# Regrouping the small-tile bursts of a fused attention and gated MLP kernel on one NeuronCore

## The chip, the cores and the metric

The kernel runs on one core of a Trainium2 chip. Five engines work beside each other, each through its own list of instructions in order: TensorE (PE, matmuls; its weight loads are listed as PEld), VectorE (DVE), ScalarE (ACT), GpSimd (POOL) and SyncE (SP, which issues DMAs; here POOL issues DMAs too). They wait for each other by semaphores. The metric is the device time of one execution in microseconds (us), lower is better. All times below are us unless they say otherwise.

## The reference

Two attentions one after the other, and then a gated layer. There are 8 batches, 8 heads, 576 rows of 64 numbers, and 32 "packed" queries p for each head.

```
packed = softmax(p k^T / 8) v           # 32 x 64 for each head
attn   = softmax(q packed^T / 8) packed # 576 x 64 for each head
x      = attn with the heads side by side      # 4608 x 512
h      = x w_in                                # 4608 x 2048
out    = (h * cos(h)) w_out                    # 4608 x 512
```

## The kernel before

All matmuls are in bf16. x is never formed. For one batch, the packed result of each head is multiplied with that head's 64 rows of w_in. That gives PPW, 256 rows (8 heads x 32 packed rows, in two halves y of 128) by 2048 columns. With a2n, the normalised second attention, h is then a2n^T PPW: a contraction over 256.

The work of one batch b has these parts, each a function:

- `s1` (L142): first scores, 16 matmuls of 64x32 tiles (L137, in `scores`), and two exponentials on ACT (L146), which write a1.
- `a1_xbar` (L158) or `a1_pe` (L163): a1 is transposed to a1T, by a DMA or by PE.
- `pp` (L173): the packed product, 48 matmuls of 96x32 tiles with 64 columns (L180); two copies take it to pp_sb. `pp_T` (L188): two transposes (L192) and a copy to ppT.
- `ppw(b, n)` (L195): 512 columns of PPW, eight matmuls of 64x32 tiles with 512 columns (L207). The result lies in a two-bank PSUM tile and is copied to PPW by the engine that is named ("evacuated"), or by two engines, one half each.
- `s2` (L221): second scores, 16 matmuls of 64x32 tiles (L137), two exponentials to a2u (L225).
- `sums2` (L228): the sums over the packed rows, two matmuls (L233), and a logarithm on ACT (L235). `normalise` (L238): exp(-log sum) on ACT (L241) and a2n on DVE (L243).
- `h_mm(b, fc)` (L248), for each of 16 groups fc of 128 columns: four matmuls of 288 columns (L254) into a two-bank tile, the cosine on ACT (L258), the product h cos h into gT on DVE (L261). I call it a step, and its fc its column.
- `out_gen` (L331): the output of a batch in chunks of 128 rows, 16 accumulating matmuls of 512 columns each (L339), a copy to osb (L343) by `osb_eng`, and DMAs on SP's queue (L345). Four chunks, or five for odd batches, whose fifth chunk holds the last 64 rows of two batches (`joint`).

The tiles of 64x32 and 96x32 use a part of the array each, so that 8 or 4 of these matmuls run side by side. All others use the whole array.

The order on each engine is the order in which the code is written (`manual_schedule`). The output matmuls of the batch before are the filler: `fill(n)` (L355) writes the next n of them wherever it is called. A slot (`slot`, L471) is the 16 steps of one batch; after each step it fills a share of the output matmuls that are left, and hooks put other work behind given columns. The argument `keep` leaves some output matmuls over, and `heavy` gives a column a larger share. `set_filler(b)` (L350) first writes out everything that is left of the batch before.

Around the slots, for batch s from 3 on (L545 to L576): what is left of the filler, `s2(s)`, ppw n=2, 8 output matmuls, `s1(s+1)`, ppw n=3, transposes by DMA, the two `sums2` with output matmuls between, `normalise`, 13 output matmuls, then the slot. In it `pp(s+1)` stands behind column 5, `pp_T(s+1)` behind column 6, and `pw2(s+1)`, which is ppw n=0 and n=1 of the next batch, behind column 10. The slots of batches 1 and 2 are laid out by hand (L496, L542), and batch 0 is a special case: its steps are `h_one` (L274), with one bank each and 512 rows; its last 64 rows are done in `h_rest` (L286), a hook in slot 1 that uses one two-bank tile for 32 matmuls, one cosine and one product over 1024 columns.

PSUM: the pool psA has three two-bank tiles, which all of s1, s2, sums2, pp, pp_T, ppw and h_mm share; the pool psO has two banks for the output chunks. Which of the three places a new tile gets is settled when the program is built, and its first matmul waits until the engines that read the old content are done. In the part of batch 0 with `h_one` psA is replaced by six single banks (psH).

ACT has two function sets, one with the exponential and logarithm, one with the cosine; `preload_act_table_set` loads one (ACT_TABLE_LOAD). Before slot 1 ACT's order is: the cosines of batch 0, the copy of ppT, the load of the set for the exponential (L449), its copy of the transposed q of batch 1 (qT, one of three groups; DVE copies the other two), then s2(1).

Of the kernel before, what the change touches and what calls it, by code (L numbers as in the profile page):

```python
# [15 lines left out]
def kernel(  # L16
# [72 lines left out]
    def psa(dt=FP32):  # L89
        return psum["A"].tile([128, 2, 512 if dt == FP32 else 1024], dt, name="psA", tag="A")  # L90
# [9 lines left out]
    def one(dt=FP32):  # L100
        return psum["H"].tile([128, 512 if dt == FP32 else 1024], dt, name="psH", tag="H")
# [56 lines left out]
    def a1_xbar(b):  # L158
        t = a1T[b] = att_pool.tile([128, 2, C, 128], BF16, name="a1T", tag="a1T")
        nc.sync.dma_start_transpose(out=t.rearrange("p a c x -> p (a c) x"),  # L160
                                    in_=a1[b % 2].rearrange("p a c x -> p (a c x)"))
# [11 lines left out]
    def pp(b, eng=V, own=None):  # L173

        ps = own() if own else psa()[:, 0, :]
        for y in range(2):
            for j in range(C):
                c = 2 * (j % 3) + j // 3
                for x in range(4):
                    nc.tensor.matmul(ps[32 * x:32 * x + 32, y * D:(y + 1) * D],  # L180
                                     a1T[b][0:TP, y, j, 32 * x:32 * x + 32],
                                     bf["v", b][:, 2 * x + y, c * D:(c + 1) * D],
                                     start=(j == 0), stop=(j == C - 1))
        t = pp_sb[b % 2].rearrange("p a d -> p (a d)")
        copy(eng, t[:, 0:2 * D], ps[:, 0:2 * D])
        copy(eng, t[:, 2 * D:3 * D], ps[:, 0:D])
# [58 lines left out]

    gT, joint = {}, {}

    def h_mm(b, fc):  # L248
        if fc == 0:
            g_tile(b)  # L250
        ps = psa()
        for y in range(2):
            for e in range(2):
                nc.tensor.matmul(ps[:, e, 0:HS], PPW[b][:, y, fc * 128:(fc + 1) * 128],  # L254
                                 a2n[b][:, y, e * HS:(e + 1) * HS], start=(y == 0), stop=(y == 1))
        cs = cos_pool.tile([128, S], BF16, name="cosT")
        csv = cs.rearrange("p (e x) -> p e x", e=2)
        ACT.activation(out=csv, in_=ps[:, :, 0:HS], func=AF.Sin, bias=PI_HALF)  # L258

        def rest():  # L260
            V.tensor_tensor(out=gT[b][:, fc, :].rearrange("p (e x) -> p e x", e=2),  # L261
                            in0=ps[:, :, 0:HS], in1=csv, op=ALU.mult)
            if fc % 8 == 7:
                j0 = (b % 2) * 64
                G.tensor_copy(out=joint[b // 2][:, fc - 7:fc + 1, j0:j0 + 64],  # L265
                              in_=gT[b][:, fc - 7:fc + 1, 512:576])
        return rest
# [3 lines left out]
        if b % 2 == 0:  # L271
            joint[b // 2] = j_pool.tile([128, NFC, 128], BF16, name="joint", tag="joint")

    def h_one(b, fc):  # L274

        if fc == 0:
            g_tile(b)
        ps = one()
        for y in range(2):
            nc.tensor.matmul(ps, PPW[b][:, y, fc * 128:(fc + 1) * 128], a2n[b][:, y, 0:512],  # L280
                             start=(y == 0), stop=(y == 1))
        cs = cos_pool.tile([128, 512], BF16, name="cosT")
        ACT.activation(out=cs, in_=ps, func=AF.Sin, bias=PI_HALF)  # L283
        V.tensor_tensor(out=gT[b][:, fc, 0:512], in0=ps, in1=cs, op=ALU.mult)  # L284

    def h_rest(b):  # L286

# [28 lines left out]
    def n_chunks(b):  # L316
        return 5 if b % 2 and b < B - 1 else 4
# [13 lines left out]
    def out_gen(b):  # L331
        groups = [(0, 1), (2,), (3,)] if b == 0 else [(c,) for c in range(n_chunks(b))]
        for grp in groups:
            pss = {c: O.tile([128, DM], FP32, name="ot", tag="ot") for c in grp}
            for f0 in range(0, NFC, 4):
                for c in grp:
                    for fc in range(f0, f0 + 4):
                        w = joint[b // 2][:, fc, :] if c == 4 else gT[b][:, fc, c * 128:(c + 1) * 128]
                        nc.tensor.matmul(pss[c], w, w_out_bf[:, fc, :],  # L339
                                         start=(fc == 0), stop=(fc == NFC - 1))  # L340
                        if fc == NFC - 1:
                            osb = o_pool.tile([128, DM], FP32, name="osb")
                            copy(osb_eng[0], osb, pss[c])  # L343
                            for a, z, rows in pieces_of(b, c):
                                nc.sync.dma_start(out=rows, in_=osb[a:z, :])  # L345
                        yield

    filler = [None, 0]

    def set_filler(b):  # L350
        fill(1000)
        filler[0] = out_gen(b)
        filler[1] = 16 * n_chunks(b)

    def fill(n):  # L355
        while n > 0 and filler[1] > 0:
            next(filler[0])
            filler[1] -= 1
            n -= 1

    def load_w_in(n):
# [11 lines left out]
    def warm(n, wps=None, w=None):  # L373
        wps, w = bank() if wps is None else wps, wz if w is None else w
        for _ in range(n):
            nc.tensor.matmul(wps, w[:, 0:128], w, start=True, stop=True)  # L376
# [60 lines left out]
    banks(0)  # L437
    a1_pe(1, own=one)
    recips(1)
    for fc in range(NFC):  # L440
        h_one(0, fc)
        if fc in (0, 4, 8):
            ppw(0, 1 + fc // 4, (ACT, ACT if fc == 8 else V), own=True)
        if fc == 13:
            pp(1, ACT, own=bank)
    warm(2)
    pp_T(1, ACT, own=bank)
    warm(2)
    ACT.preload_act_table_set(EXP_SET)  # L449
    pe_T("q", 1, (ACT, V, V), own=one)  # L450
    warm(4)
    load("v", 2)
    load("q", 2)
    load("k", 3)
# [2 lines left out]
    set_filler(0)  # L457
    s2(1)
    ppw(1, 0, V)
    fill(1)  # L460
    sums2(1, 0)
    fill(1)
    sums2(1, 1)
# [5 lines left out]
    fill(7)  # L469

    def slot(s, hooks, keep=0, heavy={}):  # L471
        left = filler[1] - keep
        weight = [1 + heavy.get(fc, 0) for fc in range(NFC)]
        for fc in range(NFC):
            h_mm(s, fc)()
            quota = (left * sum(weight[:fc + 1])) // sum(weight) - (left + keep - filler[1])
            first = quota
            while hooks and hooks[0][0] == fc:
                if first == quota and fc in heavy:
                    first = quota // 2  # L480
                    fill(first)
                hooks.pop(0)[1]()
            fill(quota - first if first != quota else quota)

    def pw2(b, n=0, eng=None):
        ppw(b, n, eng)
        ppw(b, n + 1, eng)

    def tk(n, b, i):
        return lambda: pe_T(n, b, (ACT, V, ACT), (i,))  # L490

    def cross(n, b):
        return lambda: xbar(n, b)

    osb_eng[0] = ACT
    slot(1, [(2, lambda: ppw(1, 2, (ACT, V))), (4, lambda: h_rest(0)),  # L496
             (5, lambda: ppw(1, 3, (ACT, V))), (6, lambda: pack_p(2, 4)), (8, tk("k", 2, 0)), (9, tk("k", 2, 1)),
             (9, cross("q", 2)), (10, tk("k", 2, 2)), (12, cross("k", 3))], 4, {4: 2})
    ACT.preload_act_table_set(EXP_SET)
    osb_eng[0] = V  # L500
    G.tensor_copy(out=gate, in_=xT["k", 3][0:1, 0, 0:1])
# [1 line left out]
    load("q", 3)  # L503
    load("k", 4)

    fill(1000)
    set_filler(1)
    s1(2)
    fill(7)
    a1_pe(2, (0,))  # L510
# [2 lines left out]
    recips(2)  # L513
    fill(5)
    pp(2)
    fill(2)
    pp_T(2)
    s1(3)
    a1_xbar(3)
    recips(3)  # L520
    fill(6)
    s2(2)
    ppw(2, 0, V)
    xbar("q", 3)
    xbar("k", 4)
    fill(1)
    sums2(2, 0)
    fill(3)
    sums2(2, 1)
# [7 lines left out]
    G.tensor_copy(out=gate, in_=xT["k", 4][0:1, 0, 0:1])  # L537
    for n, b in (("v", 4), ("q", 4), ("k", 5)):
        load(n, b)
    fill(9)  # L540
    osb_eng[0] = ACT
    slot(2, [(3, lambda: ppw(2, 2, (ACT, V))), (6, lambda: ppw(2, 3, (ACT, V))),  # L542
             (7, lambda: pp(3, ACT)), (8, lambda: pp_T(3, ACT)), (11, lambda: pw2(3))], 5, {11: 3})

    for s in range(3, B):  # L545
        nxt = s + 1 < B
        ACT.preload_act_table_set(EXP_SET)
        osb_eng[0] = V
        fill(1000)
        set_filler(s - 1)  # L550
        s2(s)
        ppw(s, 2, V)
        fill(8)
        if nxt:
            s1(s + 1)
            ppw(s, 3, V)
            a1_xbar(s + 1)
            xbar("q", s + 1)
            recips(s + 1)
            if s + 2 < B:  # L560
                xbar("k", s + 2)
                G.tensor_copy(out=gate, in_=xT["k", s + 2][0:1, 0, 0:1])
        else:
            ppw(s, 3, V)
        fill(4)
        sums2(s, 0)
        fill(5)
        sums2(s, 1)
        normalise(s)
        ACT.preload_act_table_set(SIN_SET)  # L570
        fill(13)
        osb_eng[0] = ACT
        for n, b in (("v", s + 2), ("q", s + 2), ("k", s + 3)):
            if b < B:
                load(n, b)
        slot(s, [(5, lambda: pp(s + 1, ACT)), (6, lambda: pp_T(s + 1, ACT)), (10, lambda: pw2(s + 1))] if nxt else [], 5, {10: 3})  # L576
    set_filler(B - 1)
    fill(1000)
    tail_chunk(B - 1, 4)
# [30 lines left out]
```

## Time and profile before

| | us |
|---|---|
| median of three runs | 249.68 (249.47 to 250.37) |
| the profiled execution | 249.53 |
| its span in the profile | 247.6 |
| PE busy, of the span | 234.0 |
| ACT busy | 170.3 |
| DVE busy | 158.5 |

The span is the time from the first to the last instruction of the program that the profile holds; some 1.9 us of the execution lie around it. The granted clock of TensorE was full throughout. In a line of a timeline stand the start, the time from the start of the first to the end of the last of its instructions, the engine, the source line, the operation, out<-in, the shape, the number of instructions, and in brackets the engine's idle time ahead of it with what ended it. Matmuls overlap: the next starts while the last drains, so the distance between starts is the cost of one, not its length. The records of some matmuls are missing in the trace, mostly the first output matmul after a burst of small tiles.

### The profile page before, as it was taken

What the parts mean: (1) busy time and instruction counts of PE and PEld (TensorE: products, weight loads), DVE (VectorE), ACT (ScalarE), POOL (GpSimd) and SP (SyncE); (2) the same over time, 40 slices, a digit from 0 to 9 for tenths busy, and PEclk for the clock granted to TensorE, in tenths of its full rate; (3) what the DMA queues carried; (4) which work ended last, traced back from release to release, by engine and by line L of the source; (5) the groups of instructions that cost most, each with busy time, mean ns of one, the idle gap of its engine ahead of it and who ended that gap; (6) DMA issues with size and microseconds to landing.
All of it is one profiled execution on the core that took longest, in us unless ns stands there. A gap on an engine that the chain in (4) does not pass through costs nothing.

```text
span 247.6 us, 5423 instructions
## 1 busy us (share of the span) xinstructions
PE 234.0 (95%) x2204; PEld 128.3 (52%) x2240; DVE 158.5 (64%) x244; ACT 170.3 (69%) x284; POOL 38.2 (15%) x61
## 2 busy tenths in 40 slices
PE   7988889999989999999999999999999999999993
PEld 3453344566445554565446554565456554665452
DVE  3369977676549777578757666578756685774000
ACT  2369998677568777888787677978886685874110
POOL 8532330200400041005000500030000000000000
PEclk9999999999999999999999999999999999999999
DMA  6999999999899999996999894989292113111123
GB/s 88 204 209 209 202 208 228 202 235 176 135 186 173 218 146 201 189 221 122 215 214 197 148 222 109 184 172 203 63 187 59 42 45 84 43 34 53 52 75 85
DMA packets 63992, 37.37 MB, mean 151 GB/s; under 512 B 36592, under 2 KB 59376, under 8 KB 63968
## 3 DMA queue, kind: packets, MB, share of 16 engines
q0 software_dynamic: 23184, 18.81, 50.0%
q1 hardware_dynamic: 40624, 18.09, 35.6%
q8 instruction: 17, 0.28, 0.5%
q10 hardware_dynamic: 160, 0.13, 0.2%
q14 instruction: 7, 0.06, 0.1%
HBM read 37.22 MB, written 9.44 MB: 188 GB/s over the span
## 4 chain that ended last, share of the span: by engine, by line
PE 82%; DMA 6%; DVE 4%; ACT 3%; issue 2%; POOL 2%; DVEq 0%; ACTq 0%; POOLq 0%
PE ot L339 48%; PE psA L254 22%; DMA w_in_bf<-in_moe_w_in_dram 6%; PE psA L207 3%; PE psA L137 2%; PE ot L325 1%; PE psA L233 1%; PE psA L180 1%; DVE gT L284 1%; PE psH L280 1%; DVE PPW L87 1%; ACT a2u L225 1%; DVE gT L261 1%; POOL kbf L94 1%; ACT L449 1%
## 5 line engine op out<-in xcount | busy, mean ns | idle before, releaser
L339 PE MATMUL ot<-w_out_bf,gT 128*128 128x512 bf16 x482 | 128.2, 379 | 2.8 <-issue 1.9
L261 DVE TENSOR_TENSOR gT<-psA,cosT 128x576 bf16<-128x576 f32 x112 | 83.5, 757 | 32.4 <-ACT cosT L258 31.5
L258 ACT ACTIVATE cosT<-psA 128x576 bf16<-128x576 f32 x112 | 73.0, 653 | 26.4 <-PE psA L254 24.8
L254 PE MATMUL psA<-a2n,PPW 128*128 128x288 bf16 x448 | 73.2, 286 | 0.0
L339 PEld LDWEIGHTS <-gT 128*128 128x128 bf16 x512 | 47.3, 98 | 43.5 <-issue 7.8
L254 PEld LDWEIGHTS <-PPW 128*128 128x128 bf16 x448 | 43.8, 98 | 30.5 <-issue 1.0
L87 DVE CAST PPW<-psA 128x1024 bf16<-128x1024 f32 (+1 forms) x25 | 26.1, 1050 | 7.7 <-PE psA L207 6.0
L87 DVE COPY osb<-ot 128x512 f32<-128x512 f32 (+1 forms) x14 | 9.4, 671 | 21.3 <-PE ot L325 17.4
L85 ACT COPY osb<-ot 128x512 f32<-128x512 f32 (+1 forms) x23 | 13.2, 575 | 13.5 <-PE ot L339 12.4
L265 POOL COPY joint<-gT 128x512 bf16<-128x512 bf16 x14 | 8.6, 617 | 88.4 <-DVE gT L261 88.4
L243 DVE SCALAR_TENSOR_TENSOR a2n<-a2u,r,lns 128x576 bf16<-128x576 bf16 x16 | 12.4, 814 | 8.1 <-ACT lns L241 8.1
L146 ACT ACTIVATE a<-psA 128x576 bf16<-128x576 f32 x16 | 10.3, 646 | 8.3 <-PE psA L137 8.3
L235 ACT ACTIVATE lns<-psA 128x576 f32<-128x576 f32 x16 | 10.3, 651 | 6.5 <-PE psA L233 5.9
L339 PE MATMUL ot<-w_out_bf,joint 128*128 128x512 bf16 x47 | 12.6, 379 | 0.1
L376 PE MATMUL ot<-wz 128*128 128x512 bf16 (+1 forms) x23 | 10.2, 548 | 2.0 <-DVE wz L390 1.7
L225 ACT ACTIVATE a2u<-psA,rs 128x576 bf16<-128x576 f32 x16 | 11.0, 738 | 1.5 <-PE psA L137 1.4
L207 PE MATMUL psA<-w_in_bf,ppT 64*32 64x512 bf16 x224 | 10.4, 380 | 0.2
L284 DVE TENSOR_TENSOR gT<-psH,cosT 128x512 bf16<-128x512 f32 x16 | 9.9, 682 | 0.4 <-ACT cosT L283 0.4
L241 ACT ACTIVATE lns<-lns 128x576 f32<-128x576 f32 x16 | 10.0, 674 | 0.0
L85 ACT CAST PPW<-psA 128x1024 bf16<-128x1024 f32 (+1 forms) x9 | 7.4, 825 | 2.8 <-PE psA L207 2.8
L283 ACT ACTIVATE cosT<-psH 128x512 bf16<-128x512 f32 x16 | 8.7, 619 | 0.9 <-issue 0.4
L280 PE MATMUL psH<-a2n,PPW 128*128 128x512 bf16 x30 | 7.9, 381 | 0.9 <-DVE PPW L87 0.6
(90 smaller groups left out, 163.8 us busy)
## 6 DMA issues: line engine op xcount, KB each, us to landing
kbf<-in_k_dram POOLq DMA_DIRECT2D x8, 576.0 KB, 13.5
vbf<-in_v_dram POOLq DMA_DIRECT2D x8, 576.0 KB, 7.4
qbf<-in_q_dram POOLq DMA_DIRECT2D x8, 576.0 KB, 10.6
out_dram<-osb SPq DMA_DIRECT2D x24, 192.0 KB, 2.8
out_dram<-osb SPq DMA_DIRECT2D x22, 128.0 KB, 2.9
w_in_bf<-in_moe_w_in_dram POOLq DMA_DIRECT2D x4, 512.0 KB, 16.6
w_out_bf<-in_moe_w_out_dram POOLq DMA_DIRECT2D x4, 512.0 KB, 21.2
out_dram<-osb SPq DMA_DIRECT2D x26, 64.0 KB, 2.1
```

The costliest lines, as they stand in the source:

```text
L85: ACT.copy(out=out, in_=in_)
L87: eng.tensor_copy(out=out, in_=in_)
L146: ACT.activation(out=a1[b % 2][:, y, :, 0:TP].rearrange("p (e m) x -> p e m x", e=2), in_=ps[y][:, :, 0:HS].rearrange("p e (m x) -> p e m ...
L207: nc.tensor.matmul(ps[y][32 * x:32 * x + 32, :], ppT[b % 2][r, 0, x, :], w_in_bf[r, x, n * 512:(n + 1) * 512], start=True, stop=True)
L225: ACT.activation(out=a2u[b][:, y].rearrange("p (e x) -> p e x", e=2), in_=ps[y][:, :, 0:HS], func=AF.Exp, scale=rs1[b][:, y:y + 1])
L243: V.scalar_tensor_tensor(out=a2n[b][:, y], in0=a2u[b][:, y], scalar=r1[b][:, y:y + 1], in1=lns[b][:, y], op0=ALU.mult, op1=ALU.mult)
L254: nc.tensor.matmul(ps[:, e, 0:HS], PPW[b][:, y, fc * 128:(fc + 1) * 128], a2n[b][:, y, e * HS:(e + 1) * HS], start=(y == 0), stop=(y == 1))
L258: ACT.activation(out=csv, in_=ps[:, :, 0:HS], func=AF.Sin, bias=PI_HALF)
L261: V.tensor_tensor(out=gT[b][:, fc, :].rearrange("p (e x) -> p e x", e=2), in0=ps[:, :, 0:HS], in1=csv, op=ALU.mult)
L280: nc.tensor.matmul(ps, PPW[b][:, y, fc * 128:(fc + 1) * 128], a2n[b][:, y, 0:512], start=(y == 0), stop=(y == 1))
L284: V.tensor_tensor(out=gT[b][:, fc, 0:512], in0=ps, in1=cs, op=ALU.mult)
L339: nc.tensor.matmul(pss[c], w, w_out_bf[:, fc, :], start=(fc == 0), stop=(fc == NFC - 1))
```

## The change

- The slots of batches 2 to 6 have one burst of small tiles: `tiled(b)` writes ppw n=2 and n=3 of the slot's own batch and then the packed product of the next batch. The packed product has no tile of its own; it is written into unused columns (288 to 512 of the second bank) of the tile of the step just done (`spare`). ACT evacuates ppw n=2; DVE takes pp_sb's two copies and then ppw n=3. Eight output matmuls (seven in slot 2) stand ahead of this burst and three behind it. `pp_T` moves to column 11, its copy on ACT as before.
- ppw n=0 and n=1 of a batch now stand with `s2` and `s1` ahead of its own slot, evacuated by DVE, where n=2 and n=3 stood; ahead of slot 7 there are n=1, 2 and 3 in a row.
- In slot 1 ppw n=2 and n=3 stand together behind column 2; `h_rest` moves from column 4 to column 5.
- Before slot 2, `s1(3)` directly follows `pp(2)`, with `pp_T(2)` three output matmuls later; the counts of output matmuls around are shifted.
- The filler is a list: `set_filler` no longer writes out what is left, and `fill` goes on into the next batch. Slots keep 5 or 13 output matmuls over, so that slots 3 to 7 have 37 each (before: 29 in slots 3, 5 and 7, 45 in slots 4 and 6); slot 2 has 29 (before 37), slot 1 has 47 (before 48). Ahead of slot 1 there are 13 (before 12).
- In batch 0's part, ACT's copies of pp_sb now follow the cosine of column 12, column 15 uses a bank of psO, ppT is copied behind cosine 13, and ACT's group of q1's transposes is copied ahead of the load of the set for the exponential. DVE copies its two groups ahead of its last product. Eight warming matmuls become seven.

The diff, cut to its core:

```
-    def h_one(b, fc):
+    def h_one(b, fc, own=None):
...
-        ps = one()
+        ps = (own or one)()
...
-    filler = [None, 0]
+    filler = []
     def set_filler(b):
-        fill(1000)
-        filler[0] = out_gen(b)
-        filler[1] = 16 * n_chunks(b)
+        filler.append([out_gen(b), 16 * n_chunks(b)])
...
-    for fc in range(NFC):
-        h_one(0, fc)
+    for fc in range(13):
+        h_one(0, fc)()()
         if fc in (0, 4, 8):
             ppw(0, 1 + fc // 4, (ACT, ACT if fc == 8 else V), own=True)
-        if fc == 13:
-            pp(1, ACT, own=bank)
-    warm(2)
+    c13 = h_one(0, 13)
+    pp(1, ACT, own=bank)
+    c13()()
+    c14 = h_one(0, 14)
+    c15 = h_one(0, 15, own=bank)
     pp_T(1, ACT, own=bank)
-    warm(2)
+    c14()()
+    rest15 = c15()
+    warm(4, one())
+    pe_T("q", 1, (ACT, V, V), (0,), own=one)
     ACT.preload_act_table_set(EXP_SET)
-    pe_T("q", 1, (ACT, V, V), own=one)
-    warm(4)
+    pe_T("q", 1, (ACT, V, V), (1, 2), own=one)
+    rest15()
+    warm(3, one())
...
     ppw(1, 0, V)
-    fill(1)
+    fill(2)
     sums2(1, 0)
...
+    def tiled(b):
+        own, later = spare[0], []
+        for n in (2, 3):
+            later += ppw(b, n, (ACT, V)[n - 2], later=True)
+        later[0]()
+        pp(b + 1, V, own=lambda: own)
+        later[1]()
...
-    slot(1, [(2, lambda: ppw(1, 2, (ACT, V))), (4, lambda: h_rest(0)),
-             (5, lambda: ppw(1, 3, (ACT, V))), (6, lambda: pack_p(2, 4)), (8, tk("k", 2, 0)), (9, tk("k", 2, 1)),
-             (9, cross("q", 2)), (10, tk("k", 2, 2)), (12, cross("k", 3))], 4, {4: 2})
+    slot(1, [(2, lambda: pw2(1, 2, (ACT, V))), (5, lambda: h_rest(0)), (6, lambda: pack_p(2, 4)), (8, tk("k", 2, 0)), (9, tk("k", 2, 1)),
+             (9, cross("q", 2)), (10, tk("k", 2, 2)), (12, cross("k", 3))], 4, {5: (3, 3)})
...
     pp(2)
-    fill(2)
-    pp_T(2)
     s1(3)
     a1_xbar(3)
+    fill(3)
+    pp_T(2)
     recips(3)
-    fill(6)
+    fill(5)
     s2(2)
     ppw(2, 0, V)
...
-    fill(1)
+    fill(3)
     sums2(2, 0)
...
-    fill(9)
+    fill(7)
     osb_eng[0] = ACT
-    slot(2, [(3, lambda: ppw(2, 2, (ACT, V))), (6, lambda: ppw(2, 3, (ACT, V))),
-             (7, lambda: pp(3, ACT)), (8, lambda: pp_T(3, ACT)), (11, lambda: pw2(3))], 5, {11: 3})
+    slot(2, [(6, lambda: tiled(2)), (11, lambda: pp_T(3, ACT))], 13, {6: (7, 3)})
...
-        fill(1000)
         set_filler(s - 1)
+        fill(5)
         s2(s)
-        ppw(s, 2, V)
+        ppw(s, 0, V)
         fill(8)
         if nxt:
             s1(s + 1)
-            ppw(s, 3, V)
+            ppw(s, 1, V)
...
         else:
-            ppw(s, 3, V)
+            for n in range(1, 4):
+                ppw(s, n, V)
...
-        slot(s, [(5, lambda: pp(s + 1, ACT)), (6, lambda: pp_T(s + 1, ACT)), (10, lambda: pw2(s + 1))] if nxt else [], 5, {10: 3})
+        slot(s, [(5, lambda: tiled(s)), (11, lambda: pp_T(s + 1, ACT))] if nxt else [],
+             5 if s % 2 else 13, {5: (5, 3)} if nxt else {})
```

More of the change, by code (lines that the diff above doesn't have):

```diff
@@ L246 @@
     gT, joint = {}, {}
+    spare = [None]
     def h_mm(b, fc):
@@ L251, in h_mm @@
         ps = psa()
+        spare[0] = ps[:, 1, HS:512]
         for y in range(2):
@@ L281, in h_one, with cos @@
                              start=(y == 0), stop=(y == 1))
-        cs = cos_pool.tile([128, 512], BF16, name="cosT")
-        ACT.activation(out=cs, in_=ps, func=AF.Sin, bias=PI_HALF)
-        V.tensor_tensor(out=gT[b][:, fc, 0:512], in0=ps, in1=cs, op=ALU.mult)
+        def cos():
+            cs = cos_pool.tile([128, 512], BF16, name="cosT")
+            ACT.activation(out=cs, in_=ps, func=AF.Sin, bias=PI_HALF)
+            return lambda: V.tensor_tensor(out=gT[b][:, fc, 0:512], in0=ps, in1=cs, op=ALU.mult)
+        return cos
     def h_rest(b):
@@ L346, in out_gen, with to_do @@
                         yield
-    filler = [None, 0]
+    filler = []
     def set_filler(b):
-        fill(1000)
-        filler[0] = out_gen(b)
-        filler[1] = 16 * n_chunks(b)
+        filler.append([out_gen(b), 16 * n_chunks(b)])
+    def to_do():
+        return sum(n for _, n in filler)
     def fill(n):
-        while n > 0 and filler[1] > 0:
-            next(filler[0])
-            filler[1] -= 1
+        while n > 0 and filler:
+            next(filler[0][0])
+            filler[0][1] -= 1
+            if filler[0][1] == 0:
+                filler.pop(0)
             n -= 1
@@ L471, in slot, with pw2 @@
     def slot(s, hooks, keep=0, heavy={}):
-        left = filler[1] - keep
-        weight = [1 + heavy.get(fc, 0) for fc in range(NFC)]
+        left = to_do() - keep
+        weight = [1 + heavy.get(fc, (0, 0))[0] for fc in range(NFC)]
         for fc in range(NFC):
             h_mm(s, fc)()
-            quota = (left * sum(weight[:fc + 1])) // sum(weight) - (left + keep - filler[1])
-            first = quota
+            quota = (left * sum(weight[:fc + 1])) // sum(weight) - (left + keep - to_do())
+            behind = min(quota, heavy[fc][1]) if fc in heavy else quota
+            fill(quota - behind)
             while hooks and hooks[0][0] == fc:
-                if first == quota and fc in heavy:
-                    first = quota // 2
-                    fill(first)
                 hooks.pop(0)[1]()
-            fill(quota - first if first != quota else quota)
-    def pw2(b, n=0, eng=None):
+            fill(behind)
+    def pw2(b, n, eng=None):
         ppw(b, n, eng)
         ppw(b, n + 1, eng)
+    def tiled(b):
[5 more added lines that the diff above has]
+        later[1]()
     def tk(n, b, i):
@@ L504 @@
     load("k", 4)
-    fill(1000)
     set_filler(1)
+    fill(4)
     s1(2)
@@ L548 @@
         osb_eng[0] = V
-        fill(1000)
         set_filler(s - 1)
+        fill(5)
         s2(s)
-        ppw(s, 2, V)
+        ppw(s, 0, V)
         fill(8)
```

## The prediction

> **What bounds the kernel now.** I read the page's parts 1 and 4 first, the busy shares and the chain that ended last. TensorE (PE) is busy for nearly all of the span and owns 82% of the chain. So time is won only where PE's stream gets shorter or where PE waits.
>
> ```profile
> PE 234.0 (95%) x2204; PEld 128.3 (52%) x2240; DVE 158.5 (64%) x244; ACT 170.3 (69%) x284; POOL 38.2 (15%) x61
> ...
> PE 82%; DMA 6%; DVE 4%; ACT 3%; issue 2%; POOL 2%; DVEq 0%; ACTq 0%; POOLq 0%
> ```
>
> Next comes PE's timeline (columns: start us, us, what), for the price of a burst of small tiles.
>
> ```profile
> 147.56 1.89 PE L339 MATMUL ot<-w_out_bf,joint 128*128 128x512 bf16 x8
> 149.38 0.44 PE L137 MATMUL psA<-qT,ppT 64*32 64x288 bf16 x16
> 149.63 0.40 PE L207 MATMUL psA<-w_in_bf,ppT 64*32 64x512 bf16 x8
> 149.96 1.90 PE L339 MATMUL ot<-w_out_bf,gT 128*128 128x512 bf16 x7
> ```
>
> Eight output matmuls last 1.89 and one lasts 0.379 (part 5), so one starts every (1.89 - 0.379)/7 = 0.216 us. An h step, four matmuls of 288 columns, starts every 0.49 (21.8% of the chain in pieces of 0.49). The first row's stream should end at 147.56 + 8 x 0.216 = 149.29; the burst starts at 149.38, an **edge** of 0.09. Eight small matmuls run side by side in 0.216, so the third row's end at 149.85; the next row starts at 149.96, an edge of 0.11. Elsewhere the leaving edge is up to 0.13. A burst thus costs some 0.22 beyond its stream. (The gap of 0.16 "<-issue" after some bursts, followed by one output matmul too few, is a missing record, not a wait.)
>
> What else can stop PE is its three two-bank tiles (psA). How long does an h step hold one?
>
> ```profile
> 41.63 0.65 PE L254 MATMUL psA<-a2n,PPW 128*128 128x288 bf16 x4
> ...
> 42.33 0.65 ACT L258 ACTIVATE cosT<-psA 128x576 bf16<-128x576 f32 x1 [0.27 <-PE psA L254]
> ...
> 43.01 0.76 DVE L261 TENSOR_TENSOR gT<-psA,cosT 128x576 bf16<-128x576 f32 x1 [0.16 <-ACT cosT L258]
> ...
> 43.35 0.41 PE L207 MATMUL psA<-w_in_bf,ppT 64*32 64x512 bf16 x8
> ```
>
> The product ends at 43.77, 2.14 after the step's start. The next view shows a step whose tile is taken over by the transposes of the packed product (L192), 2.18 later:
>
> ```profile
> 108.02 0.65 PE L254 MATMUL psA<-a2n,PPW 128*128 128x288 bf16 x4
> ...
> 110.20 0.27 PE L192 MATMUL psA<-ident,pp_sb 128*128 128x128 bf16 x2
> ```
>
> So a tile is free again **2.18 us** after its step's start, if ACT and DVE are not behind. PE was there at 110.06 and lost 0.14. What takes a tile out of turn brings the next steps closer to that limit.
>
> **The change, part by part** (plus is later; sums against the profiled execution, whose time is 249.53: 247.6 of span and 1.9 around it, 0.15 under the median of 249.68).
>
> *Bursts.* From 41 us on I count 29 bursts in the timeline and 20 in the changed order: one fewer in slot 1, one in the stretch before slot 2, three in slot 2, one in each of slots 3 to 6. That is -9 x 0.22 = -1.98. Six of the joined bursts change shape inside (64x32 to 96x32 or back). No row shows this switch. Its bounds are 0, as between L137 and L207, two lines of one shape (149.38 to 149.63 is their stream), and 0.22, a leaving and an entering edge. The nearest row is one edge, so I take 0.10: +0.6, with 0 and 1.3 as ends. The sums below have both terms in them.
>
> The Trainium skill, "TensorEngine Tiling (Array Packing)", Key Properties, says that a change of tiling mode drains TensorE. Each edge of 0.09 to 0.13 agrees, and by that rule the inner switch is an edge of its own, which leaves the sum as it is; if a switch of row size alone were none, the sum would be 0.6 lower.
>
> *q1 sooner.* Before slot 1 the chain runs over ACT:
>
> ```profile
> 33.23 0.42 ACT L85 COPY ppT<-ot 128x256 bf16<-128x256 bf16 x1
> 33.66 1.28 ACT L449 ACT_TABLE_LOAD   x1
> 34.95 0.80 ACT L85 COPY qT<-psH 128x768 bf16<-128x768 bf16 x1
> 36.24 1.37 ACT L225 ACTIVATE a2u<-psA,rs 128x576 bf16<-128x576 f32 x2 [0.48 <-PE psA L137]
> ```
>
> In the new order pp_sb's copies follow the cosine of column 12 (31.5 to 31.8), then come ACT's cosine 13, ppT's copy, cosines 14 and 15 (to 33.7). The transposes of q1 wait for its load, which lands at 33.12 as now (0.51 of PE's weight loads waits for it), so the copy by ACT is 33.7 to 34.5, the table load 34.5 to 35.8. DVE copies its two groups before the last product, at 34.0 to 35.05; the scores start at 35.1 and are read at 35.5. The table load is last: the first exponential starts at 35.81 instead of 36.24, -0.43. One more output matmul fits into PE's wait of 0.25 before L233 (37.03): -0.22. Together **-0.65**; bounds 0, if the load lands later, and -0.9, if the load of the table hid too.
>
> The Trainium skill, "ScalarE: Activation LUTs", What ACT_TABLE_LOAD costs, speaks against this: 1.28 and a drain of 1.38 at every change of set. Here the copy starts 0.01 after the load's end. By the page's 2.66 the first exponential would come at 37.2, an estimate, and this part would be a loss of about 0.7.
>
> *Slot 1.* Joined ppw takes two tiles in a row. The second is that of step 1, which starts 0.92 into the slot and whose product ends at 43.77, 3.06 in; PE comes at 2.64 (three steps of 0.49, four output matmuls, an edge, 0.22): +0.46. Then h_rest, now behind column 5:
>
> ```profile
> 46.63 1.10 PE L291 MATMUL psA<-a2n,PPW 128*128 128x64 bf16 x32
> ...
> 47.76 1.02 ACT L295 ACTIVATE cosR<-psA 128x1024 bf16<-128x1024 f32 x1 [1.15 <-PE psA L291]
> ...
> 48.82 1.23 DVE L297 TENSOR_TENSOR joint<-psA,cosR 128x1024 bf16<-128x1024 f32 x1 [1.41 <-ACT cosR L295]
> ...
> 50.10 0.28 PE L254 MATMUL psA<-a2n,PPW 128*128 128x288 bf16 x1
> ```
>
> Its tile is free 3.47 after its start. In the built order step 7 takes it, and PE is there after h_rest (0.93), three output matmuls, step 6, pack_p (0.22) and two more: 2.73. That is +0.74. k's transposes have one output matmul less between the first two: +0.11. Gone are the waits of now at 49.8 and 50.5, 0.09 and 0.17, and a burst: -0.48. **+0.83**.
>
> *Before slot 2.* Two waits of the transposes (0.12 together) go, and two edges (0.24) become a switch (0.10): **-0.26**. The idle 0.53 before L233 at 72.02 is filled by two output matmuls, but ACT's chain from the scores (70.84) to a2n (76.16) is not shortened; step 0 now waits for a2n instead. I cost this at nothing.
>
> *Slot 2* gives 8 output matmuls to the next stretch and has one between most steps. Step 3 needs step 0's product, which DVE's casts hold up to 78.62. After step 0's end at 76.45, three output matmuls (0.65) and two steps (0.98) PE comes at 78.08 and goes on at 78.67: +0.59. At column 11 pp_T waits 0.28 for step 9's tile, and step 12 waits 0.37 for step 10's, both steps being 0.71 apart. The waits of now (0.15 before step 3, 0.08 before the first ppw, 0.34 before L180) go, three bursts go for one switch (0.56), and two ppw products (0.43) leave the slot: 1.24 - 0.57 - 0.56 - 0.43 = **-0.3**.
>
> *Slots 3 to 6.* Now there are 29 or 45 output matmuls in a slot, then 37. The joined burst stalls nothing: with eight output matmuls ahead, step 5's product is done (2.18) when the packed product starts (2.85), and with three behind, the tile of ppw (evacuated by ACT in 1.0, free at 3.85) is there when step 6 comes (3.98). A margin of 0.13 covers it; each 0.1 of delay beyond costs as much a slot. But pp_T at column 11 takes step 9's tile, so step 12 takes step 10's. PE reaches it after 0.49 + 0.43 + 0.49 + 0.11 + 0.22 = 1.74 and it is free at 2.18: **+0.44 in each of four slots**. Gone are 0.04, 0.14 and 0.16 in slots 3 and 5, and 0.22 for a burst, less 0.10, in each. Sum +1.76 - 0.68 - 0.48 = **+0.6**.
>
> *Before slot 7.* Three ppw products stand in a row where one did: two come from slot 2's side of the account, +0.43. All three, and an osb copy, are evacuated by DVE (1.23 and 0.68 each); the sums' tile is the first of them. DVE is through with the copy 3.1 after the scores and with that cast at 4.3; PE comes at 4.04: +0.30. **+0.73**.
>
> DMA: what each slot needs lands ahead; nearest is a1T for batch 3 at 82.44 and its product at about 83.5. SP's queue is passed by nothing new; its transposes are issued up to 1.8 sooner.
>
> **Sum**: -0.65 + 0.83 - 0.26 - 0.3 + 0.6 + 0.73 = +0.9, rounded; I say 249.53 + 0.9 = **250.4**.
>
> **Rivals.** (1) *The new waits are not there*, because ACT and DVE run ahead or the transposes find a free tile. They sum to 1.53 in slot 1 (0.46, 0.74, and 0.33 at k's transposes), 0.39 at slot 2's step 0, 1.24 in slot 2, 1.76 and 0.30: 5.2, so 245.2. For it: DVE is busy only 64%. Against it: a free engine does not shorten the chain of 2.18, which the view at 108 us shows to bind. (2) *The switch inside a burst costs as much as two edges*, 0.22 instead of 0.10 at six places: +0.7, 251.1; from 0.19 a switch on, the result is slower by over 0.5%. For it: every change of shape seen costs an edge on each side, and the packed product also starts with weights not yet loaded. Against it: weight loads overlap within a burst (0.14 for 16). (3) *q1's copy brings nothing*, because ACT's new order is held up by a late product: +0.65, 251.05. For it: q1 lands at 33.12, just when it is wanted. Against it: DVE's products stand 0.6 apart and leave 0.3 at column 14.
>
> **How the numbers follow.** Likeliest, 250.4: 0.65. (1) 0.10. (2) 0.17. (3) 0.08. A measurement of this kernel can tell about 0.5% from no change, that is 248.43 to 250.93. (1) is faster, 0.10; (2) and (3) are slower, 0.25; the rest is the same, 0.65. The range reaches from 249.0 (switches at 0, q1 at its best, and half a microsecond of waits less) to 251.3 (both slower cases' prices with a little to spare) and leaves out (1) and the tails.
>
> **What would show it.** After: step 12 of slots 3 to 6 idle about 0.44 behind pp_T, released by DVE's product (L264); L257 in slot 1 released by L303 after some 0.7; the second ppw of slot 1 by L264; a first L225 near 35.8; L233 before slot 7 released by DVE's PPW cast; between the last L207 and the first L180 of a joined burst 0.216 + 0.10. The prediction falls if step 12 starts without idle time, or if the joined bursts show edges unlike 0.10.

## The result, and the profile after

The changed kernel takes 251.05 us (median of nine, 250.70 to 252.28) against 249.68 (median of nine, 249.41 to 250.37): a ratio of 1.0059, 95% interval 1.0040 to 1.0078. It is slower by 0.6%, and 0.65 later than the 250.4 forecast. It lies 0.12 past 250.93, from where on the prediction speaks of "slower"; the interval has that bound, a ratio of 1.005, inside, so the runs do not settle on which side of it the kernel lies. That it is slower at all is clear of the noise. The profiled execution took 250.70, the lowest of its nine, with a span of 248.9 (before: 249.53 and 247.6).

The page after, its parts 1 and 4:

```profile
PE 236.7 (95%) x2239; PEld 128.6 (52%) x2239; DVE 161.3 (65%) x254; ACT 168.1 (68%) x272; POOL 38.1 (15%) x61
...
PE 77%; DMA 7%; DVE 7%; ACT 6%; issue 1%; DVEq 0%
```

PE is still busy for 95%, but its share of the chain falls from 82% to 77%, and DVE's and ACT's grow: the chain passes from PE to them and back more often. (The busy time of before lacks some records of output matmuls, so its growth by 2.7 is no work added.) The view of PE's waits after (columns: engine, tile and line, what it waited for, us in total, times, the longest) says where:

```profile
PE psA L257 <- DVE gT L264: 1.9, 6, 0.4
...
PE psA L257 <- DVE joint L303: 0.6, 1, 0.6
...
PE psH L112 <- DMA qbf<-in_q_dram: 0.3, 1, 0.3
PE psA L257 <- DVE a2n L243: 0.3, 1, 0.3
...
PE psA L233 <- DVE PPW L87: 0.2, 1, 0.2
```

L257 is a product step (L254 before), L264 the product h cos h on DVE. Six steps wait for a product to free their tile; before, no step was in this list (the longest wait of a step then, 0.17, is too short for it). A wait is counted from the end of the matmul ahead, which drains for 0.16 beyond its place in the stream, so a wait of 0.39 costs the stream 0.55. The six cost 2.92 together.

Where the time went is best seen by stage. The marks, read from PE's timeline, are the starts of the first and of the last product matmul of each slot (the last step has four, so this mark stands 0.37 behind its start), and in the last row the end of the last matmul. A wait within a slot's first step thus counts in the stage that begins there. The output matmuls that the change moved between stages are taken out at 0.216 each:

| stage | before | after | moved output matmuls | rest | predicted |
|---|---|---|---|---|---|
| start to the packed product of batch 1 (ahead of all changes) | 30.41 | 30.15 | 0 | -0.26 | 0 |
| from there to slot 1's first step | 10.31 | 9.89 | +1 | -0.64 | -0.65 |
| slot 1, first to last step | 20.98 | 21.68 | -1 | +0.92 | +0.83 |
| to slot 2's first step | 14.29 | 13.68 | 0 | -0.61 | -0.26 |
| to slot 3's first step | 28.08 | 26.58 | -8 | +0.23 | -0.3 |
| to slot 6's last step | 96.94 | 98.05 | +1 | +0.89 | +0.6 |
| to slot 7's first step | 9.95 | 10.50 | -1 | +0.77 | +0.73 |
| to the last matmul | 32.65 | 34.38 | +8 | 0 | 0 |
| sum | 243.60 | 244.90 | 0 | +1.30 | +0.95 |

Now the lines that answer the prediction's marks. In slot 3, after, PE's timeline with DVE's and ACT's lines between:

```profile
113.63 0.65 PE L257 MATMUL psA<-a2n,PPW 128*128 128x288 bf16 x4
113.95 0.58 ACT L85 COPY osb<-ot 128x512 f32<-128x512 f32 x1
...
114.41 0.67 ACT L261 ACTIVATE cosT<-psA 128x576 bf16<-128x576 f32 x1
114.55 0.65 PE L257 MATMUL psA<-a2n,PPW 128*128 128x288 bf16 x4
...
115.04 0.27 PE L192 MATMUL psA<-ident,pp_sb 128*128 128x128 bf16 x2
...
115.11 1.57 DVE L264 TENSOR_TENSOR gT<-psA,cosT 128x576 bf16<-128x576 f32 x2 [0.27 <-ACT cosT L261]
115.16 0.38 PE L345 MATMUL ot<-w_out_bf,gT 128*128 128x512 bf16 x1
...
115.93 0.65 PE L257 MATMUL psA<-a2n,PPW 128*128 128x288 bf16 x4 [0.39 <-DVE gT L264]
```

Step 10 starts at 113.63, step 11 at 114.55, pp_T at 115.04 takes the tile that step 12 would have had, and step 12 waits for step 10's tile until the first of DVE's two products ends. It could have started at 115.16 + 0.22 = 115.38: 0.55 lost, where 0.44 was forecast. In slots 4 and 6 the loss is the 0.44 that was forecast; step 12 of slot 4:

```profile
142.88 0.65 PE L257 MATMUL psA<-a2n,PPW 128*128 128x288 bf16 x4 [0.28 <-DVE gT L264]
```

There step 10 started at 140.70, and its tile was free 2.18 later. In slots 3 and 5 an output copy on ACT (the line at 113.95) delays step 10's cosine, and with it the product, by 0.11. That copy was missing from the forecast.

Slot 1, PE alone, three lines of its timeline (the second ppw, h_rest, step 7):

```profile
43.23 0.41 PE L207 MATMUL psA<-w_in_bf,ppT 64*32 64x512 bf16 x8 [0.27 <-DVE gT L264]
...
48.30 1.10 PE L297 MATMUL psA<-a2n,PPW 128*128 128x64 bf16 x32
...
51.76 0.65 PE L257 MATMUL psA<-a2n,PPW 128*128 128x288 bf16 x4 [0.58 <-DVE joint L303]
```

The second ppw loses 0.46 (forecast 0.46) and step 7 loses 0.74 (forecast 0.74): it starts 3.46 after h_rest, which held its tile for 3.47 before.

A joined burst, PE's timeline after, in slot 3:

```profile
106.64 1.89 PE L345 MATMUL ot<-w_out_bf,gT 128*128 128x512 bf16 x8
108.46 0.63 PE L207 MATMUL psA<-w_in_bf,ppT 64*32 64x512 bf16 x16
109.02 0.56 PE L180 MATMUL psA<-vbf,a1T 96*32 96x64 bf16 x48
109.50 0.82 PE L345 MATMUL ot<-w_out_bf,gT 128*128 128x512 bf16 x3
```

Sixteen small matmuls, two rounds of eight, should last 2 x 0.216 = 0.43; the packed product starts 0.56 after they began. The inner switch costs some 0.12 here and in the other slots (taken: 0.10).

Ahead of slot 1 (after, all engines):

```profile
32.99 1.05 PEld L112 LDWEIGHTS <-qbf 96*128 96x128 bf16 x24 [0.75 <-DMA qbf<-in_q_dram]
...
33.55 0.80 ACT L85 COPY qT<-psH 128x768 bf16<-128x768 bf16 x1 [0.24 <-PE psH L112]
...
34.36 1.28 ACT L463 ACT_TABLE_LOAD   x1
...
35.66 1.37 ACT L225 ACTIVATE a2u<-psA,rs 128x576 bf16<-128x576 f32 x2
```

The copy now precedes the load of the table, and the first exponential starts at 35.66 instead of 36.24, right after the load (forecast 35.81; q1 landed 0.17 sooner in this execution).

Ahead of slot 7 (after, PE and DVE):

```profile
204.88 2.34 DVE L87 CAST PPW<-psA 128x1024 bf16<-128x1024 f32 x2
...
204.94 1.04 PE L345 MATMUL ot<-w_out_bf,gT 128*128 128x512 bf16 x4
...
206.15 0.41 PE L233 MATMUL psA<-a2u,ones_blk 128*128 128x288 bf16 x2 [0.17 <-DVE PPW L87]
```

The sums start 0.34 late, behind the first of the two casts (forecast 0.30).

### The profile page after: what moved, and what is told of

Read it like the earlier page. It is cut to its first block, busy times and chain, and to the rows that moved or that the text cites. A ratio compares the mean times of both kernels' runs of the same rounds, so it can differ in the third digit from the quotient of the medians.

```text
span 248.9 us, 5454 instructions
## 1 busy us (share of the span) xinstructions
PE 236.7 (95%) x2239; PEld 128.6 (52%) x2239; DVE 161.3 (65%) x254; ACT 168.1 (68%) x272; POOL 38.1 (15%) x61
## 4 chain that ended last, share of the span: by engine, by line
PE 77%; DMA 7%; DVE 7%; ACT 6%; issue 1%; DVEq 0%
PE ot L345 45%; PE psA L257 19%; DMA qbf<-in_q_dram 7%; DVE gT L264 4%; PE ot L385 2%; PE psA L207 2%; ACT cosT L261 2%; PE psA L137 2%; PE psA L233 2%; PE psA L180 1%; PE ot L331 1%; PE psA L112 1%; DVE PPW L87 1%; DVE osb L87 1%; ACT kT L85 1%
## 5 line engine op out<-in xcount | busy, mean ns | idle before, releaser
L345 PE MATMUL ot<-w_out_bf,gT 128*128 128x512 bf16 x512 | 133.8, 379 | 0.0
L264 DVE TENSOR_TENSOR gT<-psA,cosT 128x576 bf16<-128x576 f32 x112 | 83.5, 756 | 24.2 <-ACT cosT L261 23.5
L257 PE MATMUL psA<-a2n,PPW 128*128 128x288 bf16 x448 | 73.4, 286 | 2.8 <-DVE gT L264 1.9
L345 PEld LDWEIGHTS <-gT 128*128 128x128 bf16 x512 | 48.1, 98 | 39.6 <-issue 4.2
L257 PEld LDWEIGHTS <-PPW 128*128 128x128 bf16 x448 | 43.7, 98 | 33.7 <-issue 4.9
L87 DVE CAST PPW<-psA 128x1024 bf16<-128x1024 f32 (+1 forms) x25 | 26.8, 1090 | 5.7 <-PE psA L207 5.7
L345 PE MATMUL ot<-w_out_bf,joint 128*128 128x512 bf16 x48 | 11.9, 380 | 0.0
L385 PE MATMUL ot<-wz 128*128 128x512 bf16 (+1 forms) x17 | 8.5, 603 | 1.9 <-DVE wz L399 1.7
L85 ACT CAST PPW<-psA 128x1024 bf16<-128x1024 f32 (+1 forms) x7 | 6.1, 889 | 5.5 <-PE psA L207 5.5
L289 DVE TENSOR_TENSOR gT<-psH,cosT 128x512 bf16<-128x512 f32 x15 | 9.3, 681 | 0.4 <-ACT cosT L288 0.4
```

The source lines that it names most:

```text
L85: ACT.copy(out=out, in_=in_)
L87: eng.tensor_copy(out=out, in_=in_)
L345: nc.tensor.matmul(pss[c], w, w_out_bf[:, fc, :], start=(fc == 0), stop=(fc == NFC - 1))
```

## The experiments

The theory: the change saves what was forecast (edges of bursts, the head), and gives back more through PSUM tiles taken out of turn, whose next users wait. The rivals: the waits only move when one is taken away; the bursts themselves cost as much joined as parted; the head brings nothing.

**1. pp_T behind the last column.** The one number that puts pp_T's tile in front of step 12:

```
-    (11, lambda: pp_T(3, ACT))
+    (15, lambda: pp_T(3, ACT))
...
-    (11, lambda: pp_T(s + 1, ACT))
+    (15, lambda: pp_T(s + 1, ACT))
```

> The changed kernel with the transposes of the packed product (pp_T) behind the last column of slots 2 to 6 instead of behind column 11. Theory (new waits for PSUM tiles give back what the joined bursts save): pp_T takes a tile where only output matmuls follow, so step 12 no longer waits 0.44 to 0.55 in slots 3 to 6 and 0.38 in slot 2, and slot 2's pp_T no longer waits 0.28: 2.65 less, of which up to 0.3 may come back because ppT is copied late for the scores of the next batch: about 248.5. Rival (the waits only move to the next step, or it is the bursts themselves that cost): within 0.5 of the changed kernel, 250.5 to 251.

Measured 248.45 (248.27 to 249.22), before 249.63 beside it: ratio 0.9956 (0.9941 to 0.9971). This is 2.6 below the changed kernel and below the kernel before. PE's waits and slot 3's end in this run:

```profile
PE psA L257 <- DVE joint L303: 0.6, 1, 0.6
...
PE psA L257 <- DVE gT L264: 0.4, 1, 0.4
```

```profile
117.61 0.65 PE L257 MATMUL psA<-a2n,PPW 128*128 128x288 bf16 x4
118.10 0.28 PE L192 MATMUL psA<-ident,pp_sb 128*128 128x128 bf16 x2
118.21 1.67 PE L345 MATMUL ot<-w_out_bf,gT 128*128 128x512 bf16 x7
119.81 0.44 PE L137 MATMUL psA<-qT,ppT 64*32 64x288 bf16 x16
```

One wait for L264 is left of six (slot 2's step 3). Behind pp_T there are now seven output matmuls, which need no tile of psA, and the next scores come without idle time. By stage slot 2 and slots 3 to 6 are shorter by 0.71, 0.66, 0.55, 0.66 and 0.55, and the stretches behind them longer by 0.26 and four times 0.11: 2.43 less. The 0.11 is pp_T itself, which now stands there. Behind slot 2 its wait of 0.28 did move along with it (pp_T is at 91.59, step 13's product ends at 91.54), against the expectation, while the next ppw comes 0.13 sooner. Elsewhere the waits did not move on; the first rival falls for slots 3 to 6.

**2. Slot 1 as before, first try.**

```
-    slot(1, [(2, lambda: pw2(1, 2, (ACT, V))), (5, lambda: h_rest(0)), ...], 4, {5: (3, 3)})
+    slot(1, [(2, lambda: ppw(1, 2, (ACT, V))), (4, lambda: h_rest(0)),
+             (5, lambda: ppw(1, 3, (ACT, V))), ...], 4, {4: (2, 2)})
```

> The changed kernel with slot 1's hooks and its share of output matmuls as before (ppw 2 behind column 2, h_rest behind 4, ppw 3 behind 5). Theory: the waits at the second ppw, at step 7 and at k's transposes go (0.49 + 0.74 + 0.33 seen), one burst (0.22) and old waits (0.26) come back: 0.8 to 1.0 less than the changed kernel, 250.1. Rival (slot 1 is neutral, the waits of the joined form are hidden elsewhere): 251.

Measured 251.09 (250.64 to 252.31): no gain, a miss. Slot 1 lasted 21.72, as in the changed kernel. The edit wasn't the old slot: it put six output matmuls ahead of h_rest and two behind it, where the kernel before has four and four. In this run's timeline:

```profile
48.19 1.10 PE L297 MATMUL psA<-a2n,PPW 128*128 128x64 bf16 x32
...
51.65 0.53 PE L257 MATMUL psA<-a2n,PPW 128*128 128x288 bf16 x3 [0.57 <-DVE joint L303]
```

Step 6 comes 3.46 after h_rest and loses 0.73 on its tile: the same wait at another step. What covers h_rest's tile is what stands behind it.

**3 and 5. The head alone.** The changed part of batch 0 and the copies of q1 (the diff of the change), in the kernel before; experiment 3 also has the second output matmul behind batch 1's first ppw, experiment 5 hasn't:

```
     ppw(1, 0, V)
-    fill(1)
+    fill(2)      # experiment 3 only
```

> The kernel before with the changed head alone: the cosines 13 to 15 parted, q1's first group copied by ScalarE ahead of the table load, two output matmuls behind the first ppw of batch 1. Theory: 0.65 less than the kernel before, 249.0. Rival (q1's copy brings nothing, the first scores wait for something else): 249.7, no difference.

Measured 249.45 (248.84 to 250.58), before 249.63: ratio 0.998 (0.9960 to 1.0001). The median gains less than the 0.65 expected; the interval has both 0.65 and nothing inside. From pp(1) to slot 1's first step it took 9.48, against 10.31; but slot 1 took 21.29 with one output matmul less, against 20.98: 0.53 was given back there. The waits are 0.20 at step 0 (for a2n; none before), 0.31 before step 6 (0.09 before) and 0.32 at k's transposes (0.22 before). Hence experiment 5, whose text on record also lists step 3; the gap there is a missing record:

> The kernel before with the changed head, but with one output matmul behind batch 1's first ppw as before, not two. In the run of the changed head alone, slot 1 (first to last product step) lasted 21.29, against 20.98 in the kernel before, although it held one output matmul (0.22) less: 0.53 of new waits, at step 0, step 3, step 6 and k's transposes. Theory (the output matmul taken out of slot 1 is the one that covered those waits): slot 1 is 20.98 to 21.1 again, and the stretch from pp(1) to slot 1's first step is 0.4 to 0.8 shorter than the 10.31 of before; 249.2 in all. Rival (the earlier scores themselves upset slot 1, its a2n is later by PE's count): slot 1 stays at 21.3 or above.

Slot 1 lasted 20.98 again, and from pp(1) to slot 1 it took 9.70: both as the theory has it. (In both experiments pp(1) started 0.5 to 0.8 later than in the kernel before, so less of the time behind it went into the wait for q1's load; the 9.89 of the changed kernel is the fairer figure.) The time, 249.42 (249.07 to 250.44) beside 249.73, ratio 0.9979 (0.9958 to 1.0000), is no better than experiment 3's, so only the stages, and not the totals, tell the two apart. In its profiled execution slot 2 was longer by 1.12, by a wait that has nothing to do with the edit (last section).

**4. The joined burst parted.** One of the output matmuls of each joined burst between the two ppw and the packed product:

```
-            fill(quota - behind)
+            fill(quota - behind - (1 if fc in heavy and s > 1 else 0))
...
+        fill(1)
         later[0]()
         pp(b + 1, V, own=lambda: own)
```

> The changed kernel with one of the output matmuls of each joined burst of slots 2 to 6 put between the two ppw and the packed product, so that five switches from 64x32 to 96x32 become a leaving and an entering edge (0.12 + 0.09). Theory (an inner switch costs 0.11): 5 x 0.10 = 0.5 more, 251.5. Rival 1 (the switch costs as much as two edges): no more, 251.05. Rival 2 (the switch hides a wait that the parting covers): less than 251.05.

Measured 251.21 (251.17 to 252.61): ratio 1.0070 (1.0046 to 1.0093). The totals hardly tell 251.21 from 251.05; the stages do. Slots 2 to 6 lasted 16.57, 17.19, 17.08, 17.19 and 17.08 against 16.47, 17.08, 16.98, 17.08 and 16.97: 0.10 or 0.11 each. Slot 3's burst in this run:

```profile
109.02 0.62 PE L207 MATMUL psA<-w_in_bf,ppT 64*32 64x512 bf16 x16
109.58 0.39 PE L345 MATMUL ot<-w_out_bf,gT 128*128 128x512 bf16 x1
109.89 0.56 PE L180 MATMUL psA<-vbf,a1T 96*32 96x64 bf16 x48
```

From ppw to the output matmul 0.56 - 0.43 = 0.13, from there to the packed product 0.31 - 0.22 = 0.09: 0.22, against 0.12 for the switch. An inner switch costs somewhat over half of what two edges cost: about as much as leaving, so that joining here saves the entering edge.

**6. Slot 1's order as before**, four output matmuls on each side of h_rest (against experiment 2; slot 1 still has the 47 output matmuls of the change):

```
-             ...], 4, {4: (2, 2)})
+             ...], 4, {4: (2, 4)})
```

> The changed kernel with slot 1's hooks as before and its output matmuls parted four ahead of h_rest and four behind it, as the kernel before has them; the earlier try had six and two, and step 6 waited 0.73 there for h_rest's tile. Theory: slot 1 lasts 21.3, as with the changed head alone, against 21.68 in the changed kernel: 0.4 less, 250.65. So the joined ppw and the later h_rest cost 0.4, not 0.83, the rest being the output matmul that the head took. Rival: 21.7 again, 251.05.

Slot 1 lasted 21.19, 0.49 less than in the changed kernel. The total does not show it: 251.16 (250.27 to 252.84), ratio 1.0054 (1.0028 to 1.0079), with a spread of 2.6 us in which 0.4 is lost; the profiled execution has waits outside the edit (last section). That the joining costs slot 1 some 0.5 rests on the stage alone.

**7. Room behind what takes a tile out of turn.** On top of experiment 1:

```
-    slot(1, [..., (6, lambda: pack_p(2, 4)), (8, tk("k", 2, 0)), (9, tk("k", 2, 1)), ...
-             (10, tk("k", 2, 2)), (12, cross("k", 3))], 4, {5: (3, 3)})
+    slot(1, [..., (8, tk("k", 2, 0)), (10, tk("k", 2, 1)), (12, tk("k", 2, 2)), (12, cross("k", 3)),
+             (14, lambda: pack_p(2, 4))], 4, {2: (2, 1), 5: (3, 3)})
...
-    fill(7)
+    fill(9)
     osb_eng[0] = ACT
-    slot(2, [...], 13, {6: (7, 3)})
+    slot(2, [...], 5, {6: (7, 3)})
...
-        osb_eng[0] = V
+        osb_eng[0] = V if nxt else ACT     # back to V ahead of sums2
```

> The changed kernel with room behind whatever takes a PSUM tile out of turn: pp_T behind the last column (slots 2 to 6); in slot 1 five output matmuls ahead of the joined ppw, k's transposes behind columns 8, 10 and 12, pack_p behind 14 instead of 6; slot 2 keeps 5 output matmuls back instead of 13, and two more stand before it; before slot 7 the output copy goes to ScalarE. No burst is added. Theory: from the run with pp_T last (248.45) the waits of slot 1 (0.10, 0.46, 0.74, 0.33) fall to some 0.2, those of slot 2 (0.42, 0.54, 0.07, 0.28) to 0.4, that before slot 7 (0.34) to 0: 2.6 less, 245.9. Rival (PE's waits only move, since DVE's and ACT's chains set the pace): 247.5 to 248.5.

Measured 246.60 (246.25 to 247.35), ratio 0.9877 (0.9850 to 0.9904): it beats both kernels, the one before by 1.2%. That is 0.7 short of 245.9. Slot 1 fell from 21.68 to 20.52. Left in the profiled execution are waits of 0.21, 0.14 and 0.12 in slot 1, 0.36 at slot 2's step 3, 0.07 at pp_T behind slots 2 and 3 each, 0.18 in slot 3 (which has 8 output matmuls less, so its steps stand closer), and 0.11 before slot 7: 1.3, where 0.6 was allowed. The difference is about the 0.7 that is missing. Several edits stand in this run at once, so it does not price them one by one. PE's waits, the only line with a step in it:

```profile
PE psA L257 <- DVE gT L264: 0.2, 1, 0.2
```

**8. The same with its bursts parted**, against experiment 7:

```
-            fill(quota - behind)
+            fill(quota - behind - (2 if fc in heavy and s > 1 else 1 if fc == 2 and s == 1 else 0))
...
         for n in (2, 3):
             later += ppw(b, n, (ACT, V)[n - 2], later=True)
+            fill(1)
...
         ppw(b, n, eng)
+        fill(1)
         ppw(b, n + 1, eng)
```

> The run with room (246.60) with its bursts parted again: in slots 2 to 6 one output matmul between the two ppw and one between them and the packed product, in slot 1 one between the two ppw, all taken from those ahead, so nothing else moves. Theory (each burst costs its two edges, 0.22, also where nothing waits): slots 2 to 6 are longer by 2 x 0.22 less the inner switch of 0.11 each, 1.65, and slot 1 by 0.22: 248.45. Rival (with no waits left the edges are hidden, or the joining moves work that costs as much): 246.6 to 247.

Measured 248.43 (247.82 to 248.63), ratio 0.9948 (0.9930 to 0.9965), against 246.60. Slots 2 to 6 are longer by 0.33 or 0.34 each, 1.67 in all, as expected. Slot 1 is 20.52 in both: its edge is made up for by the 0.14 wait that goes and 0.10 less at step 0. So the bursts' edges are real cost, and the saving of the change is there. The second rival falls from this side too.

## Why the prediction was right and wrong

The mechanism was right, and most terms were right to a tenth. The forecast for the profiled execution was 0.95 more; by stage it is 1.30, or 1.56 without the 0.26 by which the execution after happened to be ahead before any changed instruction. So the waits were under-counted by some 0.6.

- *Bursts.* Edges of 0.09 in and 0.13 out, an inner switch of 0.12 instead of 0.10: right. Rival (2), a switch of 0.22, was wrong (experiment 4). The rule of the Trainium skill, "TensorEngine Tiling (Array Packing)", Key Properties, that a change of tiling mode drains TensorE, agrees with this case in that the inner switch isn't free: it costs 0.12, somewhat over half of two edges.
- *q1 sooner.* -0.65 forecast, -0.64 by stage. Rival (3) was wrong: the copy does bring the scores forward, and no late product held ACT up. What this is worth in the whole is less sure: neither experiment 3 nor 5 is clear of no change, and the landing of q1's load moves this stage from one execution to the next. What the step overlooked is that a2n, and not PE, sets when slot 1 gets going. a2n ended 4.66 after the first exponential in the kernel before (36.24 to 40.90) and 4.67 after it in the changed kernel (35.66 to 40.33). So the output matmul put into PE's wait before L233 brings nothing forward: part of that wait comes back at step 0 (0.10 in the changed kernel), and slot 1 loses a matmul that had covered waits there. Without the wait at step 0, slot 1 lasted 21.09 with 47 output matmuls in experiment 3 and 20.98 with 48 in experiment 5. The -0.22 was not won in these two, and the near match of the stage is in part chance. The table load cost 1.28 and the exponential followed it within 0.02 (34.36 + 1.28 to 35.66), and the load itself began within 0.01 of the copy's end (33.55 + 0.80 to 34.36), so the drain of 1.38 that the Trainium skill, "ScalarE: Activation LUTs", What ACT_TABLE_LOAD costs, adds to the load does not show here.
- *Slot 1.* Each wait as worked out (0.46, 0.74, 0.11 more at k's transposes); 0.92 instead of 0.83 by that 0.10.
- *Before slot 2 and slot 2.* "I cost this at nothing" was the weakest step. It said that the idle time before L233 goes and that step 0 waits for a2n instead. The idle time was 0.38 of stream, and 0.42 came at step 0. The waits in slot 2 were 0.54 at step 3 (forecast 0.59), 0.28 and 0.38 at pp_T and step 12 (forecast 0.28 and 0.37), and 0.04 at step 2, which the ledger left out. The stretch before slot 3 came out 0.13 longer: its first ppw, at 93.96, takes step 15's tile, whose product ended at 92.49 + 1.42 = 93.91, late because an output copy of 0.58 stood on ACT ahead of the cosines of steps 14 and 15. Together -0.38 instead of -0.56.
- *Slots 3 to 6.* The step that failed by size: 0.44 a slot was right in slots 4 and 6, but 0.55 in slots 3 and 5. The chain of a tile was taken as 2.18, "if ACT and DVE are not behind", and ACT was behind there, with an output copy of 0.58 at step 10. With the old waits and edges as forecast, +0.89 instead of +0.6.
- *Before slot 7.* 0.77 instead of 0.73, as worked out.
- Rival (1), that the new waits would not be there, was wrong; experiment 1 shows that they were the price: taking away one cause brings 2.43 back by stage.
- The measured 251.05 is, to the digit, the time that rival (3) gave, and close to rival (2)'s 251.1. By its time alone it would speak for them, and the prediction gave "slower" a chance through them alone. The lines and experiment 4 rule both out; that the numbers meet is chance.

The forecast added to this an execution, not a median: the profiled one after was the lowest of nine, 0.35 below the median, the one before 0.15 below. That, beside the 0.3 of the sum, is why 250.4 stands against 251.05.

## What to carry to other kernels

Work that takes a tile of a small rotating pool out of turn costs at the step that gets the tile after it, not where it stands; put it where work follows that needs no tile of that pool, and count the hold of the tile with the busiest order on each engine of its chain, not with the clean one. Joining bursts of small tiles saves real edges, but filler moved from one stage to another also uncovers the waits that it hid there. Where a change is worth less than the scatter of a run, compare stages between fixed marks of two traces: from slot 2 on they agreed to 0.01 to 0.02 us where nothing was edited, apart from the waits for a1's transposes of the next section, while the medians of these kernels could not tell 0.4 us.

## What the runs showed of the hardware that was not expected

Executions of one kernel differ at a few places and hardly elsewhere. The packed product of batch 1 starts between 30.13 and 32.16 in the ten profiled executions (their kernels are alike up to there). In the latest, TensorE's granted clock was down for a while, in a stretch that no experiment touched (experiment 2; columns: window, us, PE's busy time and instructions, granted clock, and two of the DMAs that play no part here):

```profile
10.00:18.00 8.00, 6.05 (x117) 1.00 1.29 209
18.00:22.00 4.00, 3.63 (x52) 0.70 1.24 206
22.00:26.00 4.00, 3.85 (x30) 0.88 1.24 205
26.00:30.00 4.00, 3.14 (x26) 1.00 1.32 205
```

The clock is at most part of that lateness: PE had done 6.05 us of work by 18, against 7.04 in the kernel before, and experiment 4, with 6.09 and a clock of 1.00, started at 31.12. What set the clock back is open.

The other place is the transpose of a1 by DMA, which runs beside the loads of the next batches. For batch 3 it landed 11.6 after its issue in the kernel before (70.86 to 82.44), but 14.3 and 14.5 after in the profiled executions of experiments 6 and 5, and the packed product waited. PE's timeline in experiment 6, slot 2:

```profile
82.43 0.63 PE L207 MATMUL psA<-w_in_bf,ppT 64*32 64x512 bf16 x16
83.94 0.55 PE L180 MATMUL psA<-vbf,a1T 96*32 96x64 bf16 x48 [0.89 <-DMA a1T<-a]
```

The wait is 0.89, and 1.40 in experiment 5, which has slot 2 of the kernel before. So it is not brought by the change. Experiment 6 has a second one, 0.61 in slot 3 (batch 4, landed 11.5 after its issue, against 7.2 before). How often it strikes each kernel was not measured.
